# Attention by hashed buckets: products with v three key tiles at a time, transposes three halves at a time, and a clamp column for rows without a match

## The chip, the core and the metric

The kernel runs on one core of one Trainium2 chip. The engines of that core run side by side and wait for each other through semaphores: TensorE (PE in the profile, its weight loads PEld), VectorE (DVE), ScalarE (ACT), GpSimd (POOL) and SyncE (SP, which only issues transfers). The metric is device time in microseconds (us) of one execution. Kernel before: median 622.31 us of 3 runs (621.67 to 625.53).

## The reference

Three stages, each fed by the one before it:

```
q, k, v: [2, 8, 768, 64]; proj: [64, 6]
bucket(t) = the six signs of t @ proj, as a number
scores = q @ k.T / 8; where bucket(q) != bucket(k): -1e9
scores -= max over the keys; a = exp(scores); a /= sum + 1e-9
x = (a @ v) as [1536, 512]
x = silu(x @ w_in) @ w_out                 # 512 -> 2048 -> 512
out = x; for rows with x @ w_skip > 0: out += gate * expert(x)   # 8 experts, 512 -> 1024 -> 512
```

A query none of whose keys has its bucket has -1e9 in every score; its weights all become 1/768, and its result is the mean of v. The last stage computes only the expert with the largest logit.

## The kernel before, in words

**Tiling of the attention.** The main loop (function `attention`, behind `rbs, xs = {}, {}`) runs over 96 *steps*. A step is one tile of 128 queries of one head against all 768 keys. Six steps (three query tiles, two heads) make a *unit*, which is a pair of heads and half of the queries; two units use one pair's operands. There are 16 units.

**One step.** Four matmuls write the scores S to one of two PSUM tiles (L385). K and Q are split in a high and a low part, and 24 rows more carry the buckets' bits, so that a score whose buckets differ is lowered by `BIG` or more. DVE takes the negated row maximum mx (L395). A small DVE instruction (L397) makes the pair bs from it: if the maximum tells that some key matches, the bias is mx and the scale 1, else both are 0, so that the exponentials of that row are all 1. ACT computes P = exp(scale S + bias) with the row sums (L399). Two steps later PE transposes P in two halves of three 128x128 blocks (L411, tile T in PSUM, three buffers); half 0 is copied to PT in SBUF by ACT (L414), half 1 mostly by DVE (L416).

**Products with v.** `em_PV` (L425) multiplies PT by v, one key tile of both heads at a time (each head's v fills 64 of the array's 128 columns). Before, the loop issues two key tiles (8 matmul records) behind the first half of transposes in every second step. Behind the last, ACT copies the result to x (L448). The sums are inverted on DVE (L429, L430), transposed by PE (tile rT, L436, which takes one of T's three buffers), copied by ACT (r, L438) and broadcast through DRAM to rb; POOL multiplies x by rb and splits it (`em_x`).

**Preparation.** For the next pair of heads the loop issues, at step numbers set by the lists PRE and POST, the scaling of k (L307), conversions on ACT (L317, L320), subtractions on POOL (L325, L330), the projections to buckets (pj on PE, L337, also in T's buffers) and two row transfers on SP.

**What sets the order.** Every engine takes its instructions in the order in which the Python code issues them; nothing reorders them. A function `hook`, called at the end of every step, mixes in the first work of the next stage: converting weights (L214 to L223 on ACT and DVE, splitting at L249 and L252), and at steps 97 and 101 the first two hidden products ph (L605: 12 matmuls of 512 columns), each followed by silu on ACT (g, L611), its rounding gh (L612) and on DVE the remainder gl (L613). The steps from 96 on only finish the attention. Behind the attention the MLP goes on with the products o (L648) and further ph.

Of the kernel before, what the change touches and what calls it, by code (L numbers as in the profile page):

```python
# [9 lines left out]
F32 = mybir.dt.float32  # L10
# [15 lines left out]
def kernel(  # L26
# [237 lines left out]
    def attention(hook):  # L264
# [106 lines left out]
        NS = len(steps)  # L371
        st_P, st_S, st_PT, st_sum, st_pv = {}, {}, {}, {}, {}

        def em_S(s, parts=(0, 1)):
            u, qt, hd = steps[s]
            i, qh = units[u]
            Q1, K1, Q2, K2 = ops[i]
            q0 = qh * HQ + qt * P
            if 0 in parts:
                st_S[s] = psS.tile([P, 2, 512], F32, tag="S", name="S", bufs=2)  # L380
            ps = st_S[s]
# [6 lines left out]
        def em_soft(s):  # L388
# [3 lines left out]
            ps = st_S.pop(s)  # L392
            mx = mxs[s % 4]
            bs_ = mainp.tile([P, 2], F32, name="bs", bufs=4)
# [8 lines left out]
        def em_T(s, half):  # L403
            u, qt, hd = steps[s]
            if (qt, hd, half) == (0, 0, 0):
                st_PT[u] = mainp.tile([P, 2, KT, HQ], F32, name="PT", bufs=2)
            pt = st_P[s]
            ps = psTV.tile([P, KT // 2, P], F32, tag="T", name="T", bufs=3)
            for j in range(KT // 2):
                k = half * (KT // 2) + j  # L410
                nc.tensor.transpose(ps[:, j], pt[:, k * P:(k + 1) * P], ident)  # L411
            dst = st_PT[u][:, hd, half * (KT // 2):(half + 1) * (KT // 2), qt * P:(qt + 1) * P]
            if half == 0 or NS - 2 * PU - 1 < s < NS - 1:
                nc.scalar.copy(dst, ps)  # L414
            else:
                nc.vector.tensor_copy(dst, ps)  # L416
            if half:
                del st_P[s]

        def em_PV(u, k):  # L420
            i, qh = units[u]
            if k == 0:
                st_pv[u] = psTV.tile([P, HQ], F32, tag="V", name="pv", bufs=1)
            for hd in range(2):
                nc.tensor.matmul(st_pv[u][hd * D:(hd + 1) * D], vts[i][:, k, hd], st_PT[u][:, hd, k],  # L425
                                 start=(k == 0), stop=(k == KT - 1))

# [17 lines left out]
        def em_out(u):  # L445

            x = mainp.tile([P, HQ], F32, name="x", bufs=2)
            nc.scalar.copy(x, st_pv.pop(u))  # L448
            del st_PT[u]
            return x  # L450

        def em_x(u, x, rb, eng):
# [20 lines left out]

        mxs = [mainp.tile([P, 2], F32, name=f"mx{j}", bufs=1) for j in range(4)]
        for t in mxs:
            nc.vector.memset(t, 1.0)
        nc.scalar.dma_start(ct, consts[:, 0:NC + P])
# [22 lines left out]
        for c in range(2):  # L500
# [11 lines left out]
        prep_op(0, 1, "ql", nc.gpsimd)  # L512
        prep_op(1, 0, "scale", nc.scalar)
        nc.gpsimd.memset(K2s[1][D:D + 32].bitcast(F32), 0.0)

        PRE = [[(c[j], j // 2, w, nc.scalar) for j, w in enumerate(("kh", "qa", "kh", "qa"))]
               for c in ((1, 3, 5, 7), (2, 4, 6, 8))]

        POST = [[(c[j], j // 4, w, None if w in ("k2", "qb") else nc.gpsimd)
                 for j, w in enumerate(("k2", "kl", "qb", "ql") * 2)]  # L520
                for c in ((1, 2, 3, 4, 5, 7, 7, 9), (2, 3, 4, 5, 6, 7, 8, 9))]
        rbs, xs = {}, {}
        for s in range(NS + PU + 4):
# [11 lines left out]
            w, pm = divmod(s, PU)  # L535
            u, k = (w - 1, pm - 2) if pm >= 2 else (w - 2, pm + 4)
            pv = 0 <= u < len(units)

            if pv and k % 2:
                em_PV(u, k - 1)  # L540
                em_PV(u, k)
            if s < NS:
                em_soft(s)
# [5 lines left out]
            if 0 <= s - 2 < NS:  # L549
                em_T(s - 2, 1)  # L550
            if pv:
                if k == 0:
                    em_rc(u)
                if k == (1 if u + 1 < len(units) else 3):
                    rbs[u] = em_r(u)
                if k == KT - 1:
                    xs[u] = em_out(u)
                if k == 3 and u:
                    em_x(u - 1, xs.pop(u - 1), rbs.pop(u - 1), nc.gpsimd)
            if nxt:  # L560
                if m == (1 if i else 5):
                    prep_proj(i + 1)
                for mm, *op in POST[i == 0]:
                    if mm == m:
                        prep_op(i + 1, *op)
                if m == (4 if i else 8):
                    prep_rows(i + 1)
                if m == 0 and i + 2 < B * NP:
                    prep_load(i + 2)
                if m == (9 if i else 11) and i + 2 < B * NP:  # L570
                    prep_op(i + 2, 0, "scale", nc.scalar)
# [227 lines left out]
    def hook(s):  # L799

        m = s % (2 * PU)
        if s == -6 * 2 * PU:
            pools["w0"], pools["w0_st"] = opened("w0", side="right")
            pools["stg"], pools["stg_st"] = opened("stg0", side="right")
            stage(2)
        if -5.5 * 2 * PU < s < -2 * PU and m in (2, 9, 11):
            next(early[0], None)
# [422 lines left out]
```

## Time and profile before

| | |
|---|---|
| median of 3 runs | 622.31 us |
| profiled execution | 622.04 us, its span 620.3 us |
| mean granted TensorE clock | 0.998 |
| PE, DVE, ACT, POOL busy | 97%, 75%, 65%, 27% of the span |
| share of PE in the chain that ended last | 87% |
| S matmuls (L385), transposes (L411), products with v (L425) | 92.3, 88.7, 72.3 us of PE |
| exp (L399) and copies to PT (L414) on ACT | 95.5 and 50.5 us |
| maxima (L395) and copies to PT (L416) on DVE | 91.1 and 47.0 us |

A row of the timeline gives the start from the begin of the span, the duration, the engine, the line and operation, the output and inputs, and how many like instructions stand in it; in brackets stands how long the engine was idle before it, and what released it. Durations of neighbouring matmul rows overlap, because matmuls are pipelined: what a row costs PE is the distance from its start to that of the next.

### The profile page before, as it was taken

Reading aid. Unit: us, or ns where it says so; the run is one execution under the profiler, and the core shown is the slowest. Engines: PE = TensorE matmul, PEld = TensorE weight load, DVE = VectorE, ACT = ScalarE, POOL = GpSimd, SP = SyncE. Lnnn points to the kernel's source line nnn. Section 1 sums busy time; section 2 is a strip of 40 time slices with the busy share of each in tenths; the row PEclk is TensorE's granted clock in tenths of the full one; section 3 lists DMA queues with packets and bytes.
Section 4 is the critical chain, followed back from the end, with each engine's and each line's share of the span. In section 5 each row is a group of like instructions: output and inputs, shape, how many; then the busy total and the mean of one; then the engine's idle time right before and its main releaser. Section 6 shows DMA issues by size and latency. Waiting matters only on the chain.

```text
span 620.3 us, 9579 instructions
## 1 busy us (share of the span) xinstructions
PE 604.2 (97%) x3263; PEld 463.3 (75%) x3263; DVE 465.7 (75%) x861; ACT 400.7 (65%) x671; POOL 167.3 (27%) x256
## 2 busy tenths in 40 slices
PE   8899999999999999999999999999999979999996
PEld 5767667676666757788888887788888857788885
DVE  6877777888787667799747775457885469899992
ACT  6988888888877985466554333443334456888881
POOL 5535637373653143000000000020000054534101
PEclk9999999999999999999999999999999999999999
DMA  4433542524324131666423000024232349999900
GB/s 134 144 113 93 174 124 58 157 66 137 79 66 122 46 115 52 214 216 229 143 89 121 1 1 1 1 47 164 97 103 101 118 150 257 395 408 408 391 20 28
DMA packets 30978, 83.47 MB, mean 135 GB/s; under 512 B 6032, under 2 KB 9810, under 8 KB 30798
## 3 DMA queue, kind: packets, MB, share of 16 engines
q1 hardware_dynamic: 28834, 79.06, 38.6%
q0 software_dynamic: 1936, 3.65, 1.7%
q8 instruction: 26, 0.43, 0.3%
q14 instruction: 26, 0.21, 0.1%
q10 hardware_dynamic: 156, 0.11, 0.1%
HBM read 67.66 MB, written 8.50 MB: 123 GB/s over the span
## 4 chain that ended last, share of the span: by engine, by line
PE 87%; DVE 4%; ACT 3%; DMA 2%; issue 2%; POOL 1%; SPq 0%; POOLq 0%; DVEq 0%; ACTq 0%
PE ph L605 20%; PE o L648 13%; PE S L385 11%; PE T L411 10%; PE pv L425 10%; PE o L639 7%; PE eh L1046 6%; PE ey L1068 6%; ACT P L399 1%; PE tr L1024 1%; PE pj L337 1%; DVE wlo L252 1%; PE bs L472 1%; DMA w<-in_mw_dram 1%; ACT K L317 1%
## 5 line engine op out<-in xcount | busy, mean ns | idle before, releaser
L252 DVE TENSOR_TENSOR wlo<-wraw,whi 128x1024 fp32r<-128x1024 f32 x100 | 119.6, 1222 | 5.8 <-ACT whi L249 4.9
L249 ACT CAST whi<-wraw 128x1024 fp32r<-128x1024 f32 x100 | 102.7, 1050 | 20.0 <-DVE wraw L223 13.1
L399 ACT ACTIVATE P<-S,bs 128x768 f32<-128x768 f32 x96 | 95.5, 994 | 27.1 <-DVE bs L397 25.3
L611 ACT ACTIVATE g<-ph 128x512 f32<-128x512 f32 x48 | 28.6, 597 | 119.8 <-PE ph L605 113.1
L395 DVE TENSOR_REDUCE mx<-S 128x1 f32<-128x768 f32 x96 | 91.1, 949 | 11.1 <-PE S L385 8.8
L385 PE MATMUL S<-K,Q 88*128 88x384 f32 (+1 forms) x384 | 92.3, 361 | 3.1 <-ACT P L399 3.0
L411 PEld LDWEIGHTS T<-ident,P 128*128 128x128 f32 x576 | 68.1, 141 | 30.8 <-ACT PT L414 22.1
L411 PE MATMUL T<-ident,P 128*128 128x128 f32 x576 | 88.7, 277 | 0.2 <-ACT PT L414 0.2
L613 DVE TENSOR_TENSOR gl<-g,gh 128x512 fp32r<-128x512 f32 x48 | 33.6, 701 | 68.9 <-ACT gh L612 68.9
L777 POOL DMA_INDIRECT id_d<-tk,slot x12 | 12.2, 1014 | 248.1 <-DVE pre L785 245.0
L425 PE MATMUL pv<-PT,v 128*64 128x384 f32 x384 | 72.3, 498 | 0.0
L385 PEld LDWEIGHTS S<-K,Q 88*128 88x128 f32 (+1 forms) x384 | 62.7, 191 | 11.7 <-ACT P L399 5.8
L416 DVE COPY PT<-T 128x384 f32<-128x384 f32 x85 | 47.0, 553 | 22.5 <-PE T L411 22.4
L414 ACT COPY PT<-T 128x384 f32<-128x384 f32 x107 | 50.5, 479 | 7.1 <-PE T L411 6.8
L605 PE MATMUL ph<-xhi,whi 128*128 128x512 f32 x192 | 52.9, 397 | 0.0
L605 PE MATMUL ph<-xhi,wlo 128*128 128x512 f32 x192 | 51.8, 392 | 0.7 <-DVE wlo L252 0.7
L605 PE MATMUL ph<-xlo,whi 128*128 128x512 f32 x192 | 51.9, 392 | 0.0
L325 POOL TENSOR_TENSOR K<-raw,K 64x192 fp32r<-64x192 f32 x56 | 31.6, 594 | 53.9 <-ACT K L317 28.9
L661 DVE CUSTOM_DVE_ANT_0 junk<-x,gwb 128x512 bf16<-128x512 f32 x72 | 45.4, 687 | 0.0
L330 POOL TENSOR_TENSOR Q<-raw,Q 64x192 fp32r<-64x192 f32 x64 | 36.1, 592 | 28.1 <-ACT Q L320 26.4
L605 PEld LDWEIGHTS ph<-xhi,wlo 128*128 128x128 f32 x192 | 36.0, 188 | 9.0 <-DVE wlo L252 1.2
L425 PEld LDWEIGHTS pv<-PT,v 128*64 128x64 f32 x384 | 23.4, 136 | 25.7 <-issue 25.6
(173 smaller groups left out, 1045.6 us busy)
## 6 DMA issues: line engine op xcount, KB each, us to landing
wraw<-in_w_dram SPq DMA_DIRECT2D x64, 512.0 KB
w<-in_mw_dram SPq DMA_DIRECT2D x32, 512.0 KB
v<-in_vt_dram SPq DMA_DIRECT2D x8, 384.0 KB
rb<-r_d SPq DMA_DIRECT2D x32, 96.0 KB
out_dram<-x SPq DMA_DIRECT2D x12, 256.0 KB
x_d<-x SPq DMA_DIRECT2D x11, 256.0 KB
raw<-in_kT_dram SPq DMA_DIRECT2D x7, 384.0 KB
raw<-in_qT_dram SPq DMA_DIRECT2D x7, 384.0 KB
```

Source lines behind the costliest of these rows:

```text
L249: nc.scalar.copy(hi[:, sl], t[:, sl])
L252: eng.tensor_tensor(lo[:, sl], t[:, sl], hi[:, sl].bitcast(F32), op=ALU.subtract)
L385: nc.tensor.matmul(ps[:, c, 0:HQ], q_[0:n, hd, q0:q0 + P], k_[0:n, hd, c * HQ:(c + 1) * HQ], start=first, stop=not first)
L395: nc.vector.tensor_reduce(mx[:, 0:1], ps[:, :, 0:HQ], axis=AX.XY, op=ALU.max, negate=True)
L399: nc.scalar.activation(pt.rearrange("p (a b) -> p a b", a=2), ps[:, :, 0:HQ], AF.Exp, bias=bs_[:, 0:1], scale=bs_[:, 1:2], accum_out=st_su ...
L411: nc.tensor.transpose(ps[:, j], pt[:, k * P:(k + 1) * P], ident)
L414: nc.scalar.copy(dst, ps)
L416: nc.vector.tensor_copy(dst, ps)
L425: nc.tensor.matmul(st_pv[u][hd * D:(hd + 1) * D], vts[i][:, k, hd], st_PT[u][:, hd, k], start=(k == 0), stop=(k == KT - 1))
L605: nc.tensor.matmul(p_[:, 0:c1 - c0], w[:, k * P:(k + 1) * P], x[:, k, t0 * P + c0:t0 * P + c1], start=(q == 0), stop=(q == len(ops3) - 1))
L648: nc.tensor.matmul(acc[t], g[:, (t - t0) * P:(t - t0 + 1) * P], w[:, DM:PIECE], start=(f == 0 and q == 0), stop=(f == NF - 1 and q == 2))
L661: nc.vector.tensor_tensor_reduce(junk, xts[t], pools["gwb_t"][:, c], op0=ALU.mult, op1=ALU.add, scale=1.0, scalar=0.0, accum_out=L[:, t, c ...
```

## The change

The change has five parts.

1. **Clamp column.** The two S tiles are fixed, and each gets a 385th column in either half that holds -BIG/2 once for all. The maximum (L390 of the changed kernel) reads it too. For a row without a match it is then at least -BIG/2, so that exp gives 0 everywhere. Exp takes mx as its bias and no scale; L397 and the mx tiles are gone.
2. **The mean of v.** The two PT tiles are fixed too, with 385 columns per key tile; the last holds 1e-9/768. The product with v so has 385 columns, and its last is 1e-9 times the mean of v. A copy of 128x1 on DVE (`em_none`) takes it to SBUF, and the copy to x on ACT adds it as bias.
3. **Order.** In three steps, the transposes are issued as three halves (9 matmuls) behind S of the first, none in the second, and nine behind S of the third; in the second step the products with v of three key tiles (12 records). Copies to PT are dealt out anew (96 on ACT and 96 on DVE, before 107 and 85).
4. **Places of the rest.** The scaling of k moves from ACT to POOL. PRE, POST, the projection, the conversions of weights in `hook`, the reciprocals, rT, x and `em_x` get other step numbers.
5. **Tail.** In the steps from 96 on, the products of unit 15 are issued in one group of 24 records, behind its rT.

```diff
-            nc.vector.tensor_reduce(mx[:, 0:1], ps[:, :, 0:HQ], axis=AX.XY, op=ALU.max, negate=True)
-            nc.vector.scalar_tensor_tensor(bs_, mx[:, 0:1].to_broadcast([P, 2]), BIG / 2, mx, op0=ALU.is_lt, op1=ALU.mult)
...
+            nc.vector.tensor_reduce(mx, Ss[s % 2][:, :, 0:HQ + 1], axis=AX.XY, op=ALU.max, negate=True)
...
-            nc.scalar.activation(pt.rearrange("p (a b) -> p a b", a=2), ps[:, :, 0:HQ], AF.Exp, bias=bs_[:, 0:1], scale=bs_[:, 1:2],
+            nc.scalar.activation(pt.rearrange("p (a b) -> p a b", a=2), Ss[s % 2][:, :, 0:HQ], AF.Exp, bias=mx,
...
+        PTs = [mainp.tile([P, 2, KT, HQ + 1], F32, name=f"PT{j}", bufs=1) for j in range(2)]
...
-            nc.scalar.copy(x, st_pv.pop(u))
+            nc.scalar.activation(x, st_pv.pop(u)[:, 0:HQ], AF.Identity, bias=st_none.pop(u))
...
+            nc.vector.tensor_copy(st_none[u], st_pv[u][:, HQ:HQ + 1])
...
-                nc.scalar.mul(ks, ks, SC)
+                eng.tensor_scalar(ks, ks, SC, None, op0=ALU.mult)
...
+            p, j = divmod(s, 3)
+            n0 = 6 * p - 5 + (0, 3, 3)[j]
...
             if s < NS:
                 em_S(s, (0, 1) if s else (1,))
-            if 0 <= s - 2 < NS:
-                em_T(s - 2, 0)
+            if j == 0 and s <= NS:
+                for n in range(3):
+                    em_T(n0 + n)
+            u, g = divmod(s - 10, 6)
+            if j == 1 and s < NS and u >= 0:
+                em_PV(u, (0, 1, 2) if g == 0 else (3, 4, 5))
+            if s == NS:
+                em_PV(len(units) - 2, (3, 4, 5))
+            if s == NS + 3:
+                em_PV(len(units) - 1, range(KT))
+            if j == 2 and s < NS or s == NS + 1:
+                for n in range(3):
+                    em_T(n0 + n)
+                em_C(n0, onA)
+                em_C(n0 + 1, onA)
...
+            u, g = divmod(s - 11, 6)
+            if s < NS and g == 0 and u >= 0 or s == NS + 2:
+                u = len(units) - 1 if s == NS + 2 else u
+                rbs[u] = em_r(u)
```

**Where instructions now stand.** PE in the middle of the attention, before: S, the halves of transposes T of the step before last, products pv of the unit before, the transposed sums rT.

```order
L385 MATMUL S_1680<-K1_1231,Q1_1230 128x384 x2
L385 MATMUL S_1680<-K2_103,Q2_1232 128x384 x2
L411 MATMUL T_1685<-ident_64,P_1636 128x128 x3
L425 MATMUL pv_1691<-PT_1475,v_861 64x384 x4
L411 MATMUL T_1701<-ident_64,P_1636 128x128 x3
L436 MATMUL rT_1706<-ident_64,sums_1427 6x128
L385 MATMUL S_1715<-K1_1231,Q1_1230 128x384 x2
```

The same engine and place in the changed kernel.

```order
L385 MATMUL S0_105<-K1_1154,Q1_1153 128x384 x2
L385 MATMUL S0_105<-K2_103,Q2_1155 128x384 x2
L427 MATMUL pv_1605<-PT1_108,v_806 64x385 x6
L385 MATMUL S1_106<-K1_1154,Q1_1153 128x384 x2
L385 MATMUL S1_106<-K2_103,Q2_1155 128x384 x2
L409 MATMUL T_1631<-ident_64,P_1562 128x128 x3
L409 MATMUL T_1635<-ident_64,P_1562 128x128 x3
L409 MATMUL T_1639<-ident_64,P_1598 128x128 x3
L438 MATMUL rT_1650<-ident_64,sums_1348 6x128
L385 MATMUL S0_105<-K1_1154,Q1_1153 128x384 x2
```

Three groups of three transposes stand together, six records of pv became a group by themselves between two S (three key tiles, two heads, each printed once where the profile counts two records), and rT now stands behind nine transposes.

ACT around the copy r, before: exp, copies to PT, one conversion for the next pair.

```order
L399 ACTIVATE P_1666,sums_1603<-S_1652,bs_1663 128x768
L414 COPY PT_1657<-T_1685 128x3x128
L320 CAST Q1_1589<-raw_1256 64x768
L399 ACTIVATE P_1699,sums_1603<-S_1680,bs_1696 128x768
L438 COPY r_1708<-rT_1706 6x128
L414 COPY PT_1657<-T_1720 128x3x128
```

The same place in the changed kernel.

```order
L398 ACTIVATE P_1598,sums_1515<-S1_106,mx_1595 128x768
L398 ACTIVATE P_1614,sums_1515<-S0_105,mx_1612 128x768
L419 COPY PT0_107<-T_1631 128x3x128
L419 COPY PT0_107<-T_1635 128x3x128
L398 ACTIVATE P_1647,sums_1515<-S1_106,mx_1645 128x768
L440 COPY r_1652<-rT_1650 6x128
L317 ACTIVATE K1_1491<-raw_1182 64x768
```

The two copies by ACT now stand together between two exps; r and the conversion both stand behind the second exp; before, r stood there too, and the conversion ahead of it.

PE in the tail, from the first ph on, before: the last product of unit 15 stands behind rT and the second ph.

```order
L411 MATMUL T_3022<-ident_64,P_2979 128x128 x3
L605 MATMUL ph_3037<-xhi_81,whi_2772 128x512 x4
L605 MATMUL ph_3037<-xlo_82,whi_2772 128x512 x4
L605 MATMUL ph_3037<-xhi_81,wlo_2773 128x512 x4
L425 MATMUL pv_3060<-PT_2884,v_2303 64x384 x8
L436 MATMUL rT_3079<-ident_64,sums_2840 6x128
L605 MATMUL ph_3092<-xhi_81,whi_2827 128x512 x4
L605 MATMUL ph_3092<-xlo_82,whi_2827 128x512 x4
L605 MATMUL ph_3092<-xhi_81,wlo_2828 128x512 x4
L425 MATMUL pv_3060<-PT_2884,v_2303 64x384 x4
```

In the changed kernel (L409 transposes, L427 pv, L438 rT, L641 ph):

```order
L427 MATMUL pv_2755<-PT0_107,v_2160 64x385 x6
L409 MATMUL T_2837<-ident_64,P_2788 128x128 x3
L409 MATMUL T_2841<-ident_64,P_2788 128x128 x3
L641 MATMUL ph_2855<-xhi_81,whi_2593 128x512 x4
L641 MATMUL ph_2855<-xlo_82,whi_2593 128x512 x4
L641 MATMUL ph_2855<-xhi_81,wlo_2594 128x512 x4
L438 MATMUL rT_2878<-ident_64,sums_2674 6x128
L427 MATMUL pv_2888<-PT1_108,v_2160 64x385 x12
L641 MATMUL ph_2922<-xhi_81,whi_2651 128x512 x4
L641 MATMUL ph_2922<-xlo_82,whi_2651 128x512 x4
L641 MATMUL ph_2922<-xhi_81,wlo_2652 128x512 x4
```

The products of unit 14's second half and six transposes still stand ahead of the first ph; rT of unit 15 stands directly behind it, and all of unit 15's products behind rT. On DVE the sums and reciprocals of unit 15 stand behind gl of that first ph, in both kernels.

## Rows read from the trace of the kernel before

**Rows 1.** The page: busy time; granted TensorE clock in 40 slices; chain by engine.
```profile
PE 604.2 (97%) x3263; PEld 463.3 (75%) x3263; DVE 465.7 (75%) x861; ACT 400.7 (65%) x671; POOL 167.3 (27%) x256
...
PEclk9999999999999999999999999999999999999999
...
PE 87%; DVE 4%; ACT 3%; DMA 2%; issue 2%; POOL 1%; SPq 0%; POOLq 0%; DVEq 0%; ACTq 0%
```

**Rows 2.** Lines view: making bias and scale; scaling k (busy, mean ns, idle before).
```profile
L397 DVE SCALAR_TENSOR_TENSOR bs<-mx 128x2 f32<-128x2 f32 x96 | 19.1, 199 | 7.7
...
L307 ACT ACTIVATE raw<-raw 128x768 f32<-128x768 f32 x7 | 5.9, 838 | 0.0
```

**Rows 3.** Timeline of PE, two steps in the middle of the attention.
```profile
160.84 0.55 PE L411 MATMUL T<-ident,P 128*128 128x128 f32 x3
161.14 0.94 PE L385 MATMUL S<-K,Q 128*128 128x384 f32 x4
161.92 0.82 PE L411 MATMUL T<-ident,P 128*128 128x128 f32 x6
162.50 0.95 PE L385 MATMUL S<-K,Q 128*128 128x384 f32 x4
163.29 0.49 PE L411 MATMUL T<-ident,P 128*128 128x128 f32 x3
163.71 1.51 PE L425 MATMUL pv<-PT,v 128*64 128x384 f32 x8
165.15 0.55 PE L411 MATMUL T<-ident,P 128*128 128x128 f32 x3
...
165.56 0.77 PE L385 MATMUL S<-K,Q 128*128 128x384 f32 x3
```

**Rows 4.** Timeline of PE, the first steps and one projection pj.
```profile
12.54 0.98 PE L385 MATMUL S<-K,Q 128*128 128x384 f32 x4 [1.26 <-ACT P L399]
...
16.67 0.96 PE L385 MATMUL S<-K,Q 128*128 128x384 f32 x4 [0.90 <-ACT P L399]
...
24.21 0.98 PE L385 MATMUL S<-K,Q 128*128 128x384 f32 x4 [0.85 <-ACT P L399]
...
25.60 0.94 PE L385 MATMUL S<-K,Q 128*128 128x384 f32 x4
...
37.45 0.85 PE L337 MATMUL pj<-raw,ct 128*32 128x384 f32 x8
```

**Rows 5.** Timeline of POOL in the first steps.
```profile
8.80 0.82 POOL L320 CAST Q<-raw 64x768 fp32r<-64x768 f32 x1
9.59 2.25 POOL L330 TENSOR_TENSOR Q<-raw,Q 64x192 fp32r<-64x192 f32 x4
```

**Rows 6.** Timeline of DVE: one maximum.
```profile
153.17 0.96 DVE L395 TENSOR_REDUCE mx<-S 128x1 f32<-128x768 f32 x1 [0.26 <-PE S L385]
```

**Rows 7.** Timeline of ACT: the copy r, and the exp behind that maximum.
```profile
153.46 0.24 ACT L438 COPY r<-rT 6x128 f32<-6x128 f32 x1
...
154.69 0.99 ACT L399 ACTIVATE P<-S,bs 128x768 f32<-128x768 f32 x1 [0.62 <-DVE bs L397]
```

**Rows 8.** Timeline of PE: the last S, the tail and the MLP's begin.
```profile
220.73 0.94 PE L385 MATMUL S<-K,Q 128*128 128x384 f32 x4
...
226.99 1.18 PE L605 MATMUL ph<-xhi,whi 128*128 128x512 f32 x4
...
229.94 2.80 PE L425 MATMUL pv<-PT,v 128*64 128x384 f32 x16
232.67 0.27 PE L436 MATMUL rT<-ident,sums 128*6 128x128 f32 x1
...
237.08 1.21 PE L648 MATMUL o<-whi,gh 128*128 128x512 f32 x4
...
253.75 1.20 PE L605 MATMUL ph<-xhi,wlo 128*128 128x512 f32 x4 [0.73 <-DVE wlo L252]
```

**Rows 9.** Timeline of DVE in the tail: the remainder gl.
```profile
231.39 0.69 DVE L613 TENSOR_TENSOR gl<-g,gh 128x512 fp32r<-128x512 f32 x1 [2.08 <-ACT gh L612]
```

More of the change, by code (lines that the diff above doesn't have):

```diff
@@ L371, in attention @@
         NS = len(steps)
-        st_P, st_S, st_PT, st_sum, st_pv = {}, {}, {}, {}, {}
+        st_P, st_T, st_sum, st_pv, st_none = {}, {}, {}, {}, {}
+        Ss = [psS.tile([P, 2, 512], F32, name=f"S{j}", bufs=1) for j in range(2)]
+        PTs = [mainp.tile([P, 2, KT, HQ + 1], F32, name=f"PT{j}", bufs=1) for j in range(2)]
         def em_S(s, parts=(0, 1)):
@@ L378, in em_S @@
             q0 = qh * HQ + qt * P
-            if 0 in parts:
-                st_S[s] = psS.tile([P, 2, 512], F32, tag="S", name="S", bufs=2)
-            ps = st_S[s]
+            ps = Ss[s % 2]
             for j in parts:
@@ L410, in em_T, with em_C, em_PV @@
                 k = half * (KT // 2) + j
[L411 to L416, printed above, removed]
+                nc.tensor.transpose(ps[:, j], st_P[s][:, k * P:(k + 1) * P], ident)
+            st_T[n] = ps
             if half:
                 del st_P[s]
-        def em_PV(u, k):
-            i, qh = units[u]
[L422 to L426, printed above, removed]
+        def em_C(n, copy):
+            if not 0 <= n < 2 * NS:
+                return
+            s, half = divmod(n, 2)
+            u, qt, hd = steps[s]
+            copy(PTs[u % 2][:, hd, half * (KT // 2):(half + 1) * (KT // 2), qt * P:(qt + 1) * P], st_T.pop(n))
+        def em_PV(u, ks):
+            i, qh = units[u]
+            if 0 in ks:
+                st_pv[u] = psTV.tile([P, HQ + 1], F32, tag="V", name="pv", bufs=1)
+            for k in ks:
+                for hd in range(2):
+                    nc.tensor.matmul(st_pv[u][hd * D:(hd + 1) * D], vts[i][:, k, hd], PTs[u % 2][:, hd, k],
+                                     start=(k == 0), stop=(k == KT - 1))
         def em_rc(u):
@@ L472, in em_busy @@
                 nc.tensor.matmul(bs, busy, busy, start=True, stop=True)
-        mxs = [mainp.tile([P, 2], F32, name=f"mx{j}", bufs=1) for j in range(4)]
-        for t in mxs:
-            nc.vector.memset(t, 1.0)
+        for t in Ss:
+            nc.vector.memset(t[:, :, HQ:HQ + 1], -BIG / 2)
         nc.scalar.dma_start(ct, consts[:, 0:NC + P])
@@ L529, in attention @@
                 em_S(s, (0, 1) if s else (1,))
-            if 0 <= s - 2 < NS:
-                em_T(s - 2, 0)
+            if j == 0 and s <= NS:
[13 more added lines that the diff above has]
+                em_C(n0 + 1, onA)
+            u, g = divmod(s - 15, 6)
+            if g == 0 and 0 <= u < len(units) - 1 or s == NS + 4:
+                u = min(u, len(units) - 1) if s < NS + 4 else len(units) - 1
+                xs[u] = em_out(u)
             for mm, *op in PRE[i == 0]:
@@ L534, in attention @@
                     prep_op(i + 1, *op)
[L535 to L541, printed above, removed]
-            if s < NS:
-                em_soft(s)
+            if j == 0 and s <= NS:
+                em_C(n0 + 1, onA)
+            if s < NS:
+                mx = em_max(s)
+            if j == 0 and s <= NS:
+                em_C(n0, onD)
+            if s < NS:
+                em_exp(s, mx)
+            if j == 1 and s < NS:
+                em_C(n0 - 1, onD)
+            if s == NS:
+                em_C(n0 + 2, onD)
+            if j == 2 and s < NS:
+                em_C(n0 + 2, onD)
             if s == 1:
@@ L548, in attention @@
                 em_busy(4)
[L549 to L559, printed above, removed]
+            u, g = divmod(s - 8, 6)
+            if g == 0 and 0 <= u < len(units):
+                em_rc(u)
+            u, g = divmod(s - 14, 6)
+            if g == 0 and 0 <= u < len(units) - 1:
+                em_none(u)
+            if s == NS + 3:
+                em_none(len(units) - 1)
+            u, g = divmod(s - 11, 6)
+            if s < NS and g == 0 and u >= 0 or s == NS + 2:
+                u = len(units) - 1 if s == NS + 2 else u
+                rbs[u] = em_r(u)
+            u, g = divmod(s - 17, 6)
+            if g == 0 and 0 <= u < len(units) - 1:
+                em_x(u, xs.pop(u), rbs.pop(u), nc.gpsimd)
             if nxt:
-                if m == (1 if i else 5):
+                if m == (2 if i else 5):
                     prep_proj(i + 1)
@@ L570, in attention @@
                 if m == (9 if i else 11) and i + 2 < B * NP:
-                    prep_op(i + 2, 0, "scale", nc.scalar)
+                    prep_op(i + 2, 0, "scale", nc.gpsimd)
                 if m == 11 and i + 2 < B * NP:
@@ L805, in hook @@
             stage(2)
-        if -5.5 * 2 * PU < s < -2 * PU and m in (2, 9, 11):
+        if -5.5 * 2 * PU < s < -2 * PU and m in (5, 8, 11):
             next(early[0], None)
```

29 lines of the change are left out of this document (16 added, 13 removed).

## The prediction

> **What bounds the kernel now.** I read the page first: its busy lines, the chain of waits and the line of TensorE's clock [rows 1]. PE is busy 97% of the span and holds 87% of the chain; DVE and ACT are at 75% and 65%, POOL at 27%. The clock line shows 9 in all 40 slices, which is the 2.4 GHz level. So the attention, which the change is about, is a stage of PE: what the change takes from DVE or ACT is worth only what PE waits for them there. Next come the timelines. Between the S that starts at 25.60 [rows 4] and the last S at 220.73 [rows 8] lie 195.13 us for 86 steps. What two steps need of PE is read from the starts of neighbouring rows [rows 3]: S to transposes .78; six transposes to the next S .58 (162.50 - 161.92); that S .79; three transposes to pv .42, where three cost only .30 ahead of S (161.14 - 160.84); eight pv records 1.44; three transposes .30. That is 4.31, and 43 times 4.31 is 185.3. The 15 transposed sums rT cost .11 each (from 165.15 to 165.56 there are .41 rather than .30): 1.65. The six projections pj of the stretch have .85 a row [rows 4], and I add .1 for the way in, as pv has .12: 5.7. The sum is 192.65, so all waits in these 195 us are 2.5 us. There is little to win by removing waits; the order of the PE work decides, and after it the two ends of the stage.
>
> **Part 1, the clamp column.** Without L397, 96 times 199 ns leave DVE, 19.1 us [rows 2]. The chain that this shortens: a maximum starts at 153.17 and takes .96 [rows 6], its exp starts at 154.69 [rows 7], .56 behind its end; without the small instruction some .1 to .25, so exp starts .3 earlier or a little more. In the middle this is cover for the new order and not time. The maximum over 770 instead of 768 columns is 2/768 of .96, nothing. Exp now reads one operand less, its scale. With both operands it has .99 [rows 7]; the nearest row without either is the scaling of k on ACT, as many columns in 838 ns [rows 2]. So an exp costs between .84 and .99; I take .99, as it keeps its bias and its sums. The other end, .15 in each of the 10 exps or so that PE waits for at the start and in the tail, is 1.5 us less.
>
> The Trainium skill (ScalarE: Activation LUTs, What ACT_TABLE_LOAD costs) says that each [128,1] operand of an ACTIVATE adds about 93 ns; by that, an estimate, ACT would lose 8.9 us over 96 exps, and the sum below would be about half a microsecond lower, 620.9.
>
> **Part 2, columns of the mean.** 385 for 384 columns is 1/384 of the products: one record is .161 (from the tail's 16 records, 2.73 from 229.94 to 232.67 [rows 8], and the eight above, 1.44: 1.29 / 8), 384 records are 61.8 us, the column .16 us. What the new pitch of PT costs is among the rivals. `em_none` and the bias on x are 16 small instructions each on DVE and ACT. They lie beside PE's work on the next unit, since x is wanted only when pv's buffer is used again, four steps later; without that cover, as in the tail, they cost what I count there.
>
> **Part 3, the order.** Three steps now: S .79, nine transposes .91 (three times .30), S .79, entry into pv .12, 12 records 1.93 and .15 for the way out (1.44 less 8 times .161), S .79, nine transposes .91. That is 6.39 against 1.5 times 4.31, 6.47. The saving of .08 is one pv group in three steps rather than one in two, paid back in part because the group lies between two S. 28.67 times 6.39 is 183.2, so 2.1 us less. No row shows S and pv side by side. With .1 more in each of 28 groups it is 2.8 us worse, with no entry cost 3.4 better; I take the cost that transposes have. New waits: rT needs a T buffer and stands behind nine transposes that fill all three, so it waits for the first copy by ACT, about .08 in 14 units: 1.1. pj waits likewise: .5. The third buffer of the transposes behind rT comes free by the copy r, which stands on ACT behind an exp. By the rows, counted from the S of that step: its maximum runs .99 to 1.95, exp from about 2.05 to 3.1 with its sums, r to 3.33; the third three of the transposes are due at 3.43 (S .79, T .91, rT .2, S .79, six T .6, and .1 of overlap). It fits by .1, and I put .8 in all on this and the like. Waits are 2.4 against 2.5 before, and the middle makes **-2.2** us.
>
> **Part 4, the start.** Before S of steps 2, 4 and 8 PE waits 1.26, .90 and .85 for exp [rows 4]. Exp of step 0 starts .3 earlier. The wait at step 4 is shorter by another .5, as one copy no longer stands ahead of that exp on ACT. At step 8 the third conversion for the next pair now stands behind the exp that S waits for, worth up to .75. I take **-1.5**, between 0 (if the work comes back one step later) and -2.2. The first scaling of k on POOL begins when POOL is done with pair 0, at 11.84 [rows 5], and takes between .82 (half the rows, one cast) and 2.25 (half the rows in four pieces) [rows 5]. So it ends by 14.1 at the latest; ACT needs it at about 14, behind two exps and the last conversion for pair 0. I count nothing; the dearest end is .1. The other six have half a unit.
>
> **Part 5, the tail.** Before, from the last S at 220.73 to the first o at 237.08 are 16.35 us [rows 8]. Now, counted from that S: nine transposes end at 1.70; rT of unit 14 and the transposes behind it wait for ACT as above, so unit 14's products start at 3.80; 12 records are 2.08, six transposes .6, so ph starts at 6.5. From ph to rT of unit 15 there were 5.68 us (226.99 to 232.67 [rows 8]), and they are not PE's: silu and gh come when ph ends, gl starts at 231.39 and takes .69 [rows 9], then DVE makes the sums and reciprocals. Before, 16 records of pv stood ahead of rT and filled 2.73 of it. Now rT stands directly behind ph: it starts at 12.24, while ph's 2.9 end at 9.4. **PE stands idle about 2.8 us.** Behind it stand 24 records of unit 15; they need pv's only buffer, and so x of unit 14, which stands on ACT behind `em_none` on DVE: 1.0 more. Then 24 records and .15 (4.0), the second ph 2.9, and o at 20.1: 3.8 later. One thing is given back: the ph at 253.75 waited .73 for wlo [rows 8]; its weights are loaded by SP behind the transfers of r, whose time is rT's, now .3 later, while PE is 3.8 later. So **+3.1**, bounds +2 (x is not waited for) to +4.2.
>
> **Sum:** -1.5 - 2.2 + 3.1 = -0.6 us. The profiled execution had 622.04, so 621.4; the median of the runs is .27 above it. I predict **621.5**. By the bounds of the terms the case's own range is 618.5 to 624.5.
>
> **Rivals.**
>
> *All new waits are hidden* (.12). The 2.4 of waits go, the start gives .7 more, the tail costs 2: 621.5 - 2.4 - .7 - 1.1 = 617.3; with the cheapest entry into pv 613.9. For it: ACT has 35% idle; against: two copies stand together ahead of the exp that r waits for.
>
> *Slower: the r copy is late* (.10). The place is the third buffer behind rT, the price what r is late, 14 times; it decides from .1 us on, my slack. If a conversion (.84, as the scaling [rows 2]) comes to stand ahead of that exp, r is .74 late and the kernel 10.4 us slower; if half of one, .32 and 4.5. In the middle 629. For it: S, maximum, exp, r and transposes are one chain with no spare work in between. Against: before, r stood at once behind an exp too (153.46 [rows 7]), and all waits of the stage were 2.5 us.
>
> *The clock falls in the tail's gap* (.07). Before, the attention has no wait of PE longer than 1.3 us, and all slices show 9 [rows 1, 4]. If 2.8 us of idleness bring the level of 1.2 GHz, the 24 records behind take twice their 4.0 us: 625.5. Nothing of before shows such a gap, nor a fall.
>
> *PT's pitch costs reads* (.06). A row of PT has 385 elements, so most rows begin off the places where they began. Lower bound: the column alone, .16. If each record loses the time of four to eight columns of its 384, it is 1 to 2% of 61.8 us, and 622.5. No row of before has such a pitch.
>
> The Trainium skill (SBUF — State Buffer, Specifications (TRN2)) says that cachelines have 16 bytes and that each cross to a new line pays a penalty; 385 elements are no whole number of such lines, so by it this would be so, at 97 or 98 lines for 96.
>
> *The change doesn't do what it says* (.03): the groups of three buy nothing, as each switch costs what two did. The middle gives 0: 623.7.
>
> The forecast itself has .62.
>
> **Range and chances.** A measurement of this kernel can tell about 1%, 6.2 us, from no change: faster is below 616.1, slower above 628.5. The range 617 to 626.5 holds the forecast's own range, the clock, the pitch and most of the hidden case. Faster by over 1% is half of the hidden case: .06. Slower is most of the late r, and a forecast or a clock case that is worse than its bounds: .11. The rest, .83, is within 1%.
>
> **What would show it.** In the profile after: groups of three steps 6.4 to 6.5 us apart (part 3); waits at the first S of under 1.0, .4 and .2 (part 4); r ending ahead of the third transposes behind rT; about 2.8 us of idle PE ahead of rT of unit 15 with DVE's reciprocal as releaser, and no wait for wlo near 257 (part 5). Wrong would be: a wait of .3 us or more in every unit behind rT (then 626 or more), a clock digit under 9 in the tail, or pv records of .163 us and more (the pitch).

## The result and the profile after

The changed kernel has a median of 626.83 us (623.91 to 628.28, 20 runs), the kernel before 622.38 (620.91 to 625.66, 20 runs): 1.0062 times as long, 95% interval 1.0048 to 1.0076. I had forecast 621.5 and a range up to 626.5. The kernel is 4.4 us slower where 0.9 us faster was forecast.

Its profiled execution took 623.91, the shortest of the 20. That is the first thing to read, since the 20 differ in TensorE's mean granted clock: .998 in this one, .996 in the two at 624.2 and 624.4, and .987 to .991 in eleven between 626.0 and 628.3 (the other six have .992 or .993). So this trace shows the waits, and a second trace is needed for the clock. First the page of the changed kernel: busy times, clock, chain, and exp.

```profile
PE 602.6 (97%) x3263; PEld 465.4 (75%) x3263; DVE 450.5 (72%) x790; ACT 385.0 (62%) x653; POOL 178.8 (29%) x265
...
PEclk9999999999999999999999999999999999999999
...
PE 87%; ACT 5%; DMA 3%; DVE 2%; issue 2%; POOL 1%; POOLq 0%; DVEq 0%; ACTq 0%
```
```profile
L398 ACT ACTIVATE P<-S,mx 128x768 f32<-128x768 f32 x96 | 86.7, 904 | 15.1 <-DVE mx L390 14.3
```

PE's busy time is 1.6 us less than before and DVE's 15.2 [rows 1]; the span is 1.8 longer. PE was given waits. Exp takes 904 ns instead of .99 us [rows 7].

PE's timeline of the changed kernel, at the rows that answer to [rows 4, 8]: S of steps 2, 4 and 9, the last S, the first ph, rT and the products of unit 15, the first o.

```profile
12.83 0.97 PE L385 MATMUL S<-K,Q 128*128 128x384 f32 x4
...
17.24 0.98 PE L385 MATMUL S<-K,Q 128*128 128x384 f32 x4
...
26.51 0.97 PE L385 MATMUL S<-K,Q 128*128 128x384 f32 x4
...
219.27 0.97 PE L385 MATMUL S<-K,Q 128*128 128x384 f32 x4
...
225.95 1.19 PE L641 MATMUL ph<-xhi,whi 128*128 128x512 f32 x4
...
231.51 0.27 PE L438 MATMUL rT<-ident,sums 128*6 128x128 f32 x1 [2.53 <-DVE none L456]
232.60 4.11 PE L427 MATMUL pv<-PT,v 128*64 128x385 f32 x24 [0.82 <-ACT x L450]
...
239.49 1.07 PE L684 MATMUL o<-whi,gh 128*128 128x512 f32 x4
```

Cut at these rows, the stages of all traces are (S2: S of step 2; start: to S of step 9; middle: to the last S; tail: to the first o; rest: to the end):

| kernel | S2 | start | middle | tail | rest | profiled | mean clock | median (runs) |
|---|---|---|---|---|---|---|---|---|
| before | 12.54 | 25.60 | 195.13 | 16.35 | 383.17 | 622.04 | .998 | 622.38 (20) |
| changed | 12.83 | 26.51 | 192.76 | 20.22 | 382.64 | 623.91 | .998 | 626.83 (20) |
| after_again | 10.82 | 27.36 | 192.80 | 21.92 | 382.72 | 626.58 | .993 | 626.58 (7) |
| gapfill | 12.13 | 26.10 | 192.74 | 20.25 | 383.21 | 624.17 | .999 | 624.84 (12) |
| fill_both | 10.86 | 26.07 | 192.77 | 20.23 | 382.43 | 623.28 | .999 | 623.33 (12) |
| tailfix | 10.78 | 26.98 | 192.77 | 16.64 | 382.25 | 620.42 | .994 | 619.96 (12) |
| scale_act | 12.05 | 24.86 | 192.79 | 21.93 | 382.65 | 624.01 | .996 | 623.86 (12) |
| both_fixed | 12.27 | 25.15 | 192.77 | 16.64 | 382.39 | 618.74 | .998 | 618.38 (6) |
| both_again | 10.73 | 23.55 | 192.73 | 16.64 | 382.20 | 616.96 | .998 | 617.72 (6) |
| before_clamp | 10.64 | 23.39 | 193.11 | 16.03 | 385.13 | 619.44 | .995 | 619.09 (6) |
| clamp_pool | 11.00 | 25.63 | 193.10 | 16.08 | 383.20 | 619.79 | .999 | 619.96 (12) |
| clamp_full | 12.08 | 24.82 | 193.12 | 16.25 | 384.00 | 619.98 | .999 | 619.55 (12) |
| after_bs | 11.60 | 27.19 | 200.34 | 22.22 | 382.68 | 634.21 | .993 | 634.86 (5) |

The middle and the tail came as forecast (-2.4, +3.9). The start did not: +.9, forecast -1.5. The start is to be read with S2 beside it, since S of step 2 comes early or late in executions of one kernel (both_fixed and both_again are the same kernel: 12.27 and 10.73; see the end). PE's timeline in the middle of the changed kernel:

```profile
164.17 2.16 PE L427 MATMUL pv<-PT,v 128*64 128x385 f32 x12
166.46 0.97 PE L385 MATMUL S<-K,Q 128*128 128x384 f32 x4
167.27 1.15 PE L409 MATMUL T<-ident,P 128*128 128x128 f32 x9
168.33 0.27 PE L438 MATMUL rT<-ident,sums 128*6 128x128 f32 x1
168.43 0.94 PE L385 MATMUL S<-K,Q 128*128 128x384 f32 x4
169.21 1.15 PE L409 MATMUL T<-ident,P 128*128 128x128 f32 x9
170.11 0.95 PE L385 MATMUL S<-K,Q 128*128 128x384 f32 x4
170.99 1.19 PE L427 MATMUL pv<-PT,v 128*64 128x385 f32 x6
```

The 6.82 us from pv to pv with one rT are three steps. Nine transposes take .90 to the next S (169.21 to 170.11), S .78 to .81, as counted. From pv to S are 2.29 here, where I had 2.08; that is one of four places of the stage with such a delay, and elsewhere it is 2.10 (116.79 to 118.89). Nine transposes to rT take 1.06, with the wait for the first copy in it.

### The profile page after: what moved, and what is told of

The parts are those of the page before. It is cut to its first block, busy times and chain, and to the rows that moved or that the text cites. A ratio compares the mean times of both kernels' runs of the same rounds, so it can differ in the third digit from the quotient of the medians.

```text
span 622.1 us, 9447 instructions
## 1 busy us (share of the span) xinstructions
PE 602.6 (97%) x3263; PEld 465.4 (75%) x3263; DVE 450.5 (72%) x790; ACT 385.0 (62%) x653; POOL 178.8 (29%) x265
## 4 chain that ended last, share of the span: by engine, by line
PE 87%; ACT 5%; DMA 3%; DVE 2%; issue 2%; POOL 1%; POOLq 0%; DVEq 0%; ACTq 0%
PE ph L641 21%; PE o L684 14%; PE S L385 11%; PE pv L427 9%; PE T L409 8%; PE o L675 7%; PE eh L1082 6%; PE ey L1104 6%; ACT P L398 2%; PE tr L1060 1%; DMA id_d<-tk,slot 1%; PE pj L337 1%; ACT PT L419 1%; DMA eidr<-id_d 1%; DMA raw<-in_kT_dram 1%
## 5 line engine op out<-in xcount | busy, mean ns | idle before, releaser
L390 DVE TENSOR_REDUCE mx<-S 128x1 f32<-128x770 f32 x96 | 91.9, 957 | 54.3 <-PE S L385 52.1
L249 ACT CAST whi<-wraw 128x1024 fp32r<-128x1024 f32 x100 | 102.7, 1051 | 10.6 <-PE ey L1104 2.6
L398 ACT ACTIVATE P<-S,mx 128x768 f32<-128x768 f32 x96 | 86.7, 904 | 15.1 <-DVE mx L390 14.3
L385 PE MATMUL S<-K,Q 88*128 88x384 f32 (+1 forms) x384 | 93.7, 365 | 2.2 <-ACT P L398 1.3
L409 PE MATMUL T<-ident,P 128*128 128x128 f32 x576 | 74.0, 273 | 0.3 <-ACT r L440 0.2
L427 PE MATMUL pv<-PT,v 128*64 128x385 f32 x384 | 69.0, 495 | 0.8 <-ACT x L450 0.8
L409 PEld LDWEIGHTS T<-ident,P 128*128 128x128 f32 x576 | 66.7, 140 | 3.7 <-issue 0.6
L419 ACT COPY PT<-T 128x384 f32<-128x384 f32 x96 | 42.7, 480 | 34.9 <-PE T L409 34.2
L419 DVE COPY PT<-T 128x384 f32<-128x384 f32 x96 | 52.9, 551 | 0.4 <-PE T L409 0.3
L641 PE MATMUL ph<-xhi,whi 128*128 128x512 f32 x192 | 52.9, 397 | 0.0
L641 PE MATMUL ph<-xlo,whi 128*128 128x512 f32 x192 | 51.8, 392 | 0.0
L641 PE MATMUL ph<-xhi,wlo 128*128 128x512 f32 x192 | 51.6, 391 | 0.0
L427 PEld LDWEIGHTS pv<-PT,v 128*64 128x64 f32 x384 | 24.9, 136 | 31.8 <-issue 29.8
L641 PEld LDWEIGHTS ph<-xlo,whi 128*128 128x128 f32 x192 | 36.1, 188 | 8.0
L641 PEld LDWEIGHTS ph<-xhi,wlo 128*128 128x128 f32 x192 | 36.1, 188 | 7.9
```

Of the source, the lines that this page charges most:

```text
L249: nc.scalar.copy(hi[:, sl], t[:, sl])
L390: nc.vector.tensor_reduce(mx, Ss[s % 2][:, :, 0:HQ + 1], axis=AX.XY, op=ALU.max, negate=True)
L409: nc.tensor.transpose(ps[:, j], st_P[s][:, k * P:(k + 1) * P], ident)
L419: copy(PTs[u % 2][:, hd, half * (KT // 2):(half + 1) * (KT // 2), qt * P:(qt + 1) * P], st_T.pop(n))
L641: nc.tensor.matmul(p_[:, 0:c1 - c0], w[:, k * P:(k + 1) * P], x[:, k, t0 * P + c0:t0 * P + c1], start=(q == 0), stop=(q == len(ops3) - 1))
```

## The experiments

The kernels came in three groups, each on a chip of its own with the kernel before beside it: 622.14 us in the first group, 622.30 in the second, 621.48 in the third. So kernels of different groups are compared by their distance to the kernel before. First group: what the clock and the tail cost, and the clamp alone.

**after_again**, the changed kernel unaltered.

> The changed kernel once more, for a second trace. Theory A (the clock): in most executions TensorE's granted clock falls behind the idle stretch of PE ahead of rT of unit 15, so the mean granted clock is .987 to .993 and the time 625.5 to 628; in the trace the granted clock is below 1 in a stretch that begins behind that rT, and the matmul rows there last about twice as long as in the first trace. Theory B (work only): the clock has nothing to do with the gap; where the mean clock is low, the low stretch lies elsewhere (the start, the last stage), and the tail reads as in the first trace.

Measured 626.58, 1.006 times before (1.0039 to 1.0082). PE's timeline in the second trace, start and tail:

```profile
10.82 0.97 PE L385 MATMUL S<-K,Q 128*128 128x384 f32 x4 [0.92 <-ACT P L398]
...
16.85 0.98 PE L385 MATMUL S<-K,Q 128*128 128x384 f32 x4 [2.38 <-ACT P L398]
18.11 1.27 PE L385 MATMUL S<-K,Q 128*128 128x384 f32 x4 [0.27 <-ACT P L398]
19.17 2.12 PE L409 MATMUL T<-ident,P 128*128 128x128 f32 x9
21.23 1.20 PE L337 MATMUL pj<-raw,ct 128*32 128x384 f32 x8
...
232.41 0.27 PE L438 MATMUL rT<-ident,sums 128*6 128x128 f32 x1 [2.53 <-DVE none L456]
233.50 5.80 PE L427 MATMUL pv<-PT,v 128*64 128x385 f32 x24 [0.82 <-ACT x L450]
239.23 1.19 PE L641 MATMUL ph<-xhi,whi 128*128 128x512 f32 x4
```

The clock of this trace by microseconds (start and end, PE and other engines' busy time, and before the last two columns, DMA, the granted clock):

```profile
18.00:19.00 1.00, 0.89 (x4) 0.90 (x5) 1.00 (x2) 0.12 (x2) 0.81 (x2) 0.78 0.81 258
19.00:20.00 1.00, 1.00 (x6) 0.91 (x5) 0.88 (x2) 0.93 (x2) 0.00 (x0) 0.50 0.37 132
...
21.00:22.00 1.00, 1.00 (x10) 0.20 (x8) 0.56 (x1) 1.00 (x3) 0.02 (x1) 0.51 0.00 0
...
233.00:234.00 1.00, 0.50 (x2) 0.23 (x4) 0.62 (x1) 1.00 (x2) 0.48 (x1) 0.80 0.07 19
...
236.00:237.00 1.00, 1.00 (x6) 0.48 (x4) 0.00 (x0) 0.00 (x0) 0.44 (x1) 0.50 0.60 160
237.00:238.00 1.00, 1.00 (x8) 0.43 (x6) 0.00 (x0) 0.00 (x0) 0.00 (x0) 0.99 0.78 254
```

It falls to .50, the 1.2 GHz level, twice: at 18.6, behind a wait of 2.38 us and 1.4 us of work, and at 233.6, behind idle stretches of 2.53 and .82. The nine transposes at 19.17 take 2.06 to the next row, and in the first trace .9 to 1.1; the 24 products take 5.73 (233.50 to 239.23), in the first trace 4.04. That is 1.69 us at the tail. The two waits of the tail are in both traces; the 2.38 ahead of S of step 4 are not in the first, where S of step 2 came 2 us later. Theory A holds for the tail, and there is a second place, the start, which theory A had not named (B had, in place of the tail). Its wait is explained by ACT and POOL of this trace:

```profile
11.71 0.84 ACT L317 ACTIVATE K<-raw 64x768 fp32r<-64x768 f32 x1
15.08 0.84 ACT L317 ACTIVATE K<-raw 64x768 fp32r<-64x768 f32 x1 [2.53 <-POOL raw L307]
```

```profile
9.85 2.96 POOL L330 TENSOR_TENSOR Q<-raw,Q 64x192 fp32r<-64x192 f32 x4
12.90 2.14 POOL L307 TENSOR_SCALAR raw<-raw 128x768 f32<-128x768 f32 x1
```

ACT's second conversion needs scaled k of pair 1. It was free at 12.55 and waited 2.53 us for POOL, whose scaling runs 12.90 to 15.04, behind four pieces that took 2.96 here and 2.25 before [rows 5]. The exp that S of step 4 waits for stands behind that conversion on ACT.

**gapfill** keeps PE at work in the tail's idle stretch, with matmuls of 128 bf16 columns on a zero tile:

```diff
+                if s == NS + 2:
+                    em_fill(44)
                 rbs[u] = em_r(u)
+                if s == NS + 2:
+                    em_fill(14)
```

> The changed kernel with 44 matmuls of 128 bf16 columns on a zero tile between the first ph and rT of unit 15, and 14 more between rT and the products of unit 15; they shorten nothing, they only keep PE at work (58 of .056 us are 3.2 us, the length of the idle stretch). Theory A: the clock stays up, mean granted clock .996 to .998, and the time falls by about 3 us, to 623.5 to 624.5. Theory B: no gain, 626.8 or a little more.

Measured 624.84, 1.7 less than the changed kernel beside it (626.58). PE's timeline:

```profile
228.40 2.63 PE L437 MATMUL fill<-busy 128*128 128x128 bf16 x44
231.09 0.27 PE L443 MATMUL rT<-ident,sums 128*6 128x128 f32 x1
231.20 0.94 PE L437 MATMUL fill<-busy 128*128 128x128 bf16 x14
232.18 4.11 PE L427 MATMUL pv<-PT,v 128*64 128x385 f32 x24
236.22 1.20 PE L650 MATMUL ph<-xhi,whi 128*128 128x512 f32 x4
```

rT stands as far behind ph as in the first trace (5.56), the products come 1.09 behind it as there, and they take 4.04 at full clock. Work without any use shortened the kernel by what the low clock had cost: A is shown, B has fallen. I had expected 1.2 us more of it; fill_both below shows where most of it is left, at the start.

**tailfix** issues three things on DVE and ACT one step earlier, ahead of the first silu, and takes them out of their old places (not shown):

```diff
+            if s == NS + 1:
+                em_rc(len(units) - 1)
+                em_none(len(units) - 2)
+                xs[len(units) - 2] = em_out(len(units) - 2)
```

> The changed kernel with the reciprocals of unit 15, the copy of the mean column of unit 14 and x of unit 14 issued one step earlier, ahead of the first ph's silu and remainder on ACT and DVE; the order on PE stays. The idle stretch of 2.5 and .8 us ahead of and behind rT goes. Theory A: these 3.3 us and about 3 us of low clock go; the wait for wlo may come back with up to .7: 620.5 to 621.3, which is 1 to 2 us less than the kernel before. Theory B: only the 3.3 us go: 623.5 to 624.2.

Measured 619.96, .9961 times before (.9944 to .9977), a little under what A gave. PE's timeline: last S, rT, products, o.

```profile
219.75 0.97 PE L385 MATMUL S<-K,Q 128*128 128x384 f32 x4
...
229.30 0.27 PE L438 MATMUL rT<-ident,sums 128*6 128x128 f32 x1
229.50 4.11 PE L427 MATMUL pv<-PT,v 128*64 128x385 f32 x24
...
236.39 1.07 PE L688 MATMUL o<-whi,gh 128*128 128x512 f32 x4
```

rT stands directly behind ph (228.38 and .92) and does not wait. The tail is 16.64 instead of 20.2 to 21.9. The wait for wlo that before had (.73 [rows 8]) did not come back; rT is 9.55 behind the last S and was 11.94, which I take to be why, though no run tests it.

**before_clamp** is the old order with L397 gone and exp with mx alone; rows without a match become zero.

> The kernel before with the clamp column alone: two fixed S tiles with the column, the maximum reads it, exp takes mx as bias and no scale, and the small DVE instruction is gone (96 times 199 ns). It leaves out the mean of v for rows without a match, which become zero. By the prediction's part 1 and 4: exp starts .3 us earlier at the first steps and is some .1 shorter, so 0.5 to 1.5 us less than before, 621 to 622. Rival: PE's order sets the time and the first waits go to something else: no change, 622.4.

Measured 619.09, .994 times before (.9918 to .9961). Two rows of PE: S of steps 4 and 9.

```profile
14.55 0.97 PE L386 MATMUL S<-K,Q 128*128 128x384 f32 x4 [0.56 <-ACT P L397]
...
23.39 0.95 PE L386 MATMUL S<-K,Q 128*128 128x384 f32 x4
```

That is 3.05 below before, where I had expected 0.5 to 1.5. The middle is 2.0 shorter, which I had given to the new order. The start is 2.2 shorter in these two traces, but that is not all the clamp's: 1.9 of it lie ahead of S of step 2 (10.64 and 12.54), .4 of them in its wait (.91 instead of 1.26) and most of the others because the first matmuls ran at full speed sooner (see the end). clamp_full, whose S of step 2 comes late too (12.08), has S of step 9 at 24.82, .8 below before; that is what the clamp gives at the start.

Second group: the two causes apart and together, and the order without the clamp.

**scale_act**: `prep_op(1, 0, "scale", nc.scalar)`, the other six scalings on POOL.

> The changed kernel with the first scaling of k (pair 1) back on ACT; the other six stay on POOL. Theory P (POOL's scaling): in the second trace of the changed kernel it ran 12.90 to 15.04, ACT waited 2.53 us for it with the second conversion, and so did exp and the S of step 4 (2.38); by that S of step 9 starts at 23.4 to 24.2 instead of 26.5 to 27.4, the clock has no reason to fall there, and the time is 623.2 to 624.2. Theory Q (the order of the first steps, three halves of transposes and the conversions in other places, makes the start late): S of step 9 stays behind 25.6, the time above 625.5.

Measured 623.86, 2.7 to 3.0 below the changed kernel (626.58 and 626.83). S of step 4 starts at 15.59 instead of 16.85. S of step 9 is at 24.86 and not by 24.2: the first S came late in this execution (see the end); from S of step 2 to that of step 9 there are 12.81 us, in after_again 16.54. P is shown, Q is not needed.

**both_fixed**: tailfix and scale_act.

> The changed kernel with the tail's instructions on ACT and DVE issued one step earlier (as in tailfix) and the first scaling on ACT. If the two causes add up: S of step 9 at 23.4 to 24.2, 192.8 to the last S, 16.6 to the first o, 382.3 to 383.2 to the end: 615.2 to 616.8 span, 617.0 to 618.6 us, below the kernel with the clamp alone (619.1). If that kernel's gain is all there is in the change, it stays at 619 or more.

Measured 618.38, .9921 times before (.9898 to .9943). The causes add up: within the expected 617.0 to 618.6, although S of step 9 is at 25.15 here, as the first S came late; in both_again it is at 23.55.

**fill_both**: gapfill and `em_busy(40)` ahead of S of step 4.

> The changed kernel with dummy matmuls in both idle stretches: those of gapfill in the tail, and 40 more of 128 bf16 columns ahead of the S of step 4, about 2.2 us. They shorten no wait. Theory A (the clock falls behind both waits and costs about 1.7 us each time): mean granted clock .997 or more in all executions and a narrow spread of times, 623.0 to 624.5, median about 623.8, against gapfill's 623.2 to 626.0 with a median of 624.84. Otherwise, if the start's low clock costs nothing in the end: the spread and median of gapfill.

Measured 623.33, all 12 between 623.11 and 624.60, mean clock .999 in the trace. Against 626.6 to 626.8 of the changed kernel the low clock so costs 3.3 to 3.5 us at both places, 1.7 in the tail and 1.5 at the start by the medians; from S of step 4 to that of step 9 there are 9.26 here (16.81 to 26.07) and 10.51 in after_again.

**after_bs**: the new order with the small DVE instruction and exp's scale put back.

> The changed kernel with the small DVE instruction for bias and scale put back and exp taking both again (the clamp column is not read, the mean column is zero): the new order without the clamp. Theory O (the prediction's part 3: PE's order makes the middle, waits are as before): from S of step 9 to the last S 192.8 to 193.3. Theory C (the clamp makes it: without it the waits for exp come back, 2 us and more, as the old order with the clamp took 193.10): 194.5 or more, and more still if the longer chain makes r late behind exp, 14 times .5. The time: 627 by O, 629 or more by C.

Measured 634.86, 1.0207 times before (1.0177 to 1.0236). The middle is 200.34, 7.6 longer than the changed kernel's. One S of it:

```profile
172.90 0.98 PE L385 MATMUL S<-K,Q 128*128 128x384 f32 x4 [0.30 <-ACT P L400]
```

Such waits for exp are 2.2 us in nine places by the waits view. Compared start by start with the changed kernel, 3.0 us of the 7.6 lie between transposes behind rT, where the last three need the buffer that the copy r frees, .1 to .4 in each of 14 units; 1.0 lies ahead of rT, and the rest mostly ahead of S. PE and ACT at one such place:

```profile
119.01 1.39 PE L411 MATMUL T<-ident,P 128*128 128x128 f32 x9
```

```profile
119.57 0.24 ACT L442 COPY r<-rT 6x128 f32<-6x128 f32 x1
```

r ends at 119.81, and the last three transposes start at 119.86, .19 later than in an unbroken row; the nine of the changed kernel take 1.15. O has fallen: without the earlier exp the new order is slower than the old one.

Third group: the failed step by itself, and what the order is worth.

**clamp_pool**: before_clamp with the first scaling on POOL.

> The kernel before with the clamp alone (as before_clamp, the mean of v left out) and the first scaling of k moved to POOL: the step that the prediction counted at nothing, by itself in the old order. Theory P: POOL begins it at 11.8 to 12.9, it takes 2.14, so the S of step 4 starts at 16.5 to 16.9 instead of 14.55; where the first S come early this is a wait of 2 us and more and the clock falls behind it: 1.5 to 4 us above before_clamp's 619.1, so 620.6 to 623. Rival: the loss at the start belongs to the new order: 619.1.

Measured 619.96, .9978 times before (.9963 to .9992), or 1.5 us below it, where before_clamp is 3.05 below the kernel before of its own group: the scaling costs 1.5. The plain difference of the two medians, .9, holds the chip's share, since the kernel before is .7 shorter on this chip. PE's S of steps 2 and 4:

```profile
11.00 0.97 PE L389 MATMUL S<-K,Q 128*128 128x384 f32 x4 [0.91 <-ACT P L400]
...
16.78 0.98 PE L389 MATMUL S<-K,Q 128*128 128x384 f32 x4 [2.45 <-ACT P L400]
```

The wait is there (2.45), in the old order too, and S of step 4 is at 16.78. The clock did not fall in this trace, and the loss is at the low end of what I expected. Eight of the twelve times are 619.5 to 620.0 and four 621.0 to 621.6; a fall in those four would explain it, and three of them have the lowest mean clock of the twelve, .996, but none was traced.

**clamp_full**: the old order with the clamp and the mean of v complete, and **both_again** beside it.

> The kernel before in its old order with the clamp and with the mean of v in full (PT tiles with 385 columns, the copy of the last column, x with a bias): parts 1 and 2 of the change without 3 to 5. The column is .16 us, the copies lie beside other work; with the 0.2 of the prediction's part 2: 619.2 to 619.6. If the pitch of 385 costs 1 to 2% of the products (the rival): 619.9 to 620.5, with pv records of .163 and more.

> both_fixed once more (618.38 in its first six runs), beside clamp_full on the same chip: what the new order of parts 3 to 5 is worth once the scaling and the tail are mended. By the traces the middle differs by 0.3 (192.78 against 193.10), the start and tail by less than 1: 0 to 1.5 us below clamp_full. Rival: nothing is left of the order, both within 0.3.

Measured 619.55 and 617.72. The products of clamp_full with their pitch of 385, by the lines view:

```profile
L425 PE MATMUL pv<-PT,v 128*64 128x385 f32 x384 | 72.5, 499 | 0.0
```

A record has 499 ns, before 498: the pitch costs nothing. The mended new order is 1.8 us below the old one with the clamp, a little more than expected. By the traces it gains .4 in the middle, and 1.8 in the rest, where the old order waits 1.4 for wlo and the new one not; the tail gives .4 back, and from S of step 2 to that of step 9 both take 12.7 to 12.8. So most of the gain is a wait of the next stage and not the order of the attention; that wait was .6 to .8 in the other traces of the old order.

## Why the prediction was wrong, point by point

**The failed step is part 4's scaling on POOL**: "I count nothing; the dearest end is .1." The duration was bounded rightly in the first and the second trace (2.14, between .82 and 2.25; in gapfill's it was 2.90). What failed is the time at which it was due. I took "about 14" from a trace in which the first S came late. ACT was free for its second conversion at 13.92 in gapfill's trace, where they came late again, but at 12.55 in after_again, where they came early, and there POOL's own pieces ahead of the scaling took 2.96 and not 2.25 (2.96 to 2.98 in each of the six traces with S2 at 11.0 or less, 2.24 to 2.26 in the others; why is open). S of step 4 now starts at 16.7 to 17.2 in all traces with that scaling, however early the first S come. With the clock's fall behind this wait the start is 1.8 above before (after_again), and was to be 1.5 below. scale_act gives 2.7 to 3.0 us back. The -1.5 itself was too much: with the scaling on ACT again and a late S of step 2, as in the trace of before, S of step 9 is at 24.86 and 25.15, only .5 to .7 below before.

**The second term that the sum had at nothing is the clock; as a rival it had .07.** Of the 5.3 us between 621.5 and 626.83 the clock is 3.3 to 3.5 (fill_both), 1.7 of it in the tail; without it the kernel has 623.3, within the forecast's own range. Together the scaling with the fall behind it, and the fall in the tail, make 4.4 to 5.0 of the 5.3. By the mean clock it fell in most executions. Its place was as named, its price too high: half speed lasted 3.4 us of the 24 records, not all, 1.69 instead of 4.0. I had put weight on "Nothing of before shows such a gap, nor a fall", but before had no such gap; absence of a row was no evidence. Executions of the kernel before that ran later have mean clocks down to .989 (624.06 us), so it does not always keep the high clock either; where it fell there was not traced.

**Part 5, the tail, held**: 3.87 by the first trace (forecast 3.8), PE idle 2.53 before rT and .82 behind it (2.8 and 1.0), and the wait for wlo gone. The view names the copy of the mean column as releaser, which on DVE stands directly behind the reciprocal that I had named.

**Part 3 had the right number for a wrong reason.** The middle fell by 2.4 (forecast 2.2), but the old order with the clamp has 193.11: 2.0 of it are gone without any new order. 1.85 of these lie ahead of S in 11 places where exp was late, part of the 2.5 I had listed and meant to be replaced by new ones; one of them, at the weight load of S, in the trace of before:

```profile
103.38 0.65 PEld L385 LDWEIGHTS S<-K,Q 128*128 128x128 f32 x4 [0.23 <-ACT P L399]
```

The order of PE itself is worth .35. And the slower rival's mechanism, r late for the third buffer behind rT, is what after_bs shows, with 3.0 us of its 7.6; the clamp is what keeps it away.

**Part 1**: exp's .99 was the wrong end; 904 ns is .09 less. The Trainium skill's rule of about 93 ns for each [128,1] operand (ScalarE: Activation LUTs, What ACT_TABLE_LOAD costs) agrees with it: 994 ns with two such operands, 904 with one. The trace of before had told no more than .84 to .99; ten exps at .09 would have been .9, and not the half microsecond that the prediction put beside that rule. **Part 2** held in the middle (193.12 with the mean of v, 193.11 without), and the rival of the pitch fell: 499 against 498 ns. By their distances to before clamp_full gains 1.93 and before_clamp 3.05, with intervals that overlap, so what part 2 costs in all is not settled (1.1 by the medians). The Trainium skill's sentence on cachelines (SBUF — State Buffer, Specifications (TRN2)) does not show in PE's reads here; the same row gives full bandwidth from two hits in a line on, so it said less for the rival than the prediction took from it.

Summed by the traces of before and after_again: start +1.76, middle -2.33, tail +5.57, rest -.45: 4.55, and 626.58 is 4.54 above 622.04. A slip of the prediction's last step is small beside this: 621.4 and the .27 by which the median is longer make 621.7, not 621.5.

## What to carry to other kernels

Before a step goes to an idle engine, ask when its result is due once the change itself has made the waiting engine faster, and what that engine has ahead of it: its mean load says nothing of the first microseconds. Price an idle stretch of PE twice, as the stretch and as half speed behind it, and look at the mean granted clock of many executions and not of the one profiled. Changes that come together need a run each: here one part gave 3 us, two hid it, and mended they give nearly 4.

## What was not expected of the hardware

The clock falls after a wait as short as 2.4 us, and not always: behind 2.38 it did in after_again, behind 2.45 in clamp_pool it did not. In before_clamp's last stage it fell behind shorter waits, of .69 and 1.16 us with one small matmul between them, at 508.9, and stayed at .50, the 1.2 GHz level, until 512.3; the rest of that trace is 385.13 long, clamp_pool's 383.20. PE there, and one microsecond of the clock:

```profile
506.71 0.28 PE L984 MATMUL gp<-ident,gat 128*12 128x128 f32 x1 [0.69 <-DVE gat L912]
508.14 0.66 PE L1021 MATMUL tr<-ident,xg 128*128 128x128 f32 x4 [1.16 <-DMA xg<-x_d,eid]
```

```profile
510.00:511.00 1.00, 1.00 (x4) 0.74 (x3) 1.00 (x2) 0.00 (x0) 0.11 (x3) 0.50 0.27 76
```

The first matmuls run at half speed, with a granted clock of 1.00 in the rows, and full speed comes at different times. The dummy matmuls ahead of the first S are .107 us apart and then .056: from 3.7 on in before_clamp and tailfix, behind 9.7 in the trace of before, and only behind 12.0 in the changed kernel's first trace, where PE had waited .41 for k at 4.3. In the kernels with the clamp S of step 2 so starts at 10.6 to 11.0 or at 12.0 to 12.8, which is most of what the start differs by between executions of like kernels. What decides it I did not test.
